# Linear attention and a gated FFN on one core: blocks 4 and 5 get all their scalings on ScalarE, with loads and casts dealt anew

## The chip, the cores and the metric

The kernel runs on one core of a Trainium2 chip. The core has TensorE (PE in the profile; PEld is its loading of weights), VectorE (DVE), ScalarE (ACT), GpSimd (POOL) and SyncE (SP), which here only issues DMAs. Each engine runs its own instructions in order; semaphores tie the engines together. The metric is device time of one launch in microseconds (us), lower is better. Runs before: 319.34, 318.82 and 317.79 us, median 318.82.

## The reference

Eight batches of eight heads, 576 positions, head size 64, in float32. The attention is linear: q and k are clipped at zero and scaled by a cosine and a sine of the position, side by side, so that a head has 128 features.

```
def phi(x, c, s):
    r = np.maximum(x, 0.0)
    return np.concatenate([r * c, r * s], axis=-1)
kv = np.einsum('bhsf,bhsd->bhfd', k_p, v)
z = np.sum(k_p, axis=2)
num = np.einsum('bhsf,bhfd->bhsd', q_p, kv)
den = np.einsum('bhsf,bhf->bhs', q_p, z)[..., None] + 1e-06
return (num / den)
```

Its result, as 4608 tokens of 512 numbers, goes through a gated FFN with 1536 hidden columns: `(gelu(x @ w_gate) * (x @ w_val)) @ w_out`.

## The kernel before, in words

**Two rhythms.** Attention goes by batch (576 tokens, eight batches b), the FFN by block of 512 tokens (nine blocks n). While block n's FFN runs on PE, the attention of batch n + 1 is made in its gaps, and the loading and scaling of batch n + 2. Block n has 12 units `jt`, each 128 hidden columns; a loop over n and jt calls the helpers in an order written out by hand (the scheduler is off), so that the order of calls is the order on each engine.

**A batch's way.** SP loads q, k and v of a batch into the staging tile `st` (`load`, L98), as 128 partitions x 4 head pairs m x 9 position columns j x 64. Each column j is then scaled twice, with the cosine table (part 0, "c") and the sine table (part 1, "s"), into the bf16 tile `phis`: `prep` for one name (L177 on ACT, L179 on DVE) or `prep_both` for q and k in one instruction (L191 on ACT, L193 on DVE). v is cast into `vx` (`cast_v`, L208). From batch 2 on, two DMA transposes (`turn_q`, L222), one for each half of the partitions, turn the scaled q into `qT`. `kv_unit` (L270) makes the key-value sums. `nm_unit` (L311, then DVE at L322 to L324) makes the numerators of 128 positions, divides them and writes `x_sb`; even and odd heads read the two halves of `qT`, so it needs both transposes. `turn_x` (L378) turns x by DMA into the FFN's input `xT`.

**Staging.** `st` has three places. From batch 4 on, q and k of the next batch land on top of those of the last, so a load of columns waits until these columns of the batch before have been scaled. q of batch 4 has its own load at slot (2, 1), in two halves by head pair.

**The FFN.** Up to block 3 a unit is `gv_unit` (L430): gate matmuls into one PSUM bank, value matmuls into another, a Gelu on ACT (L439) and a product on DVE (L442). Blocks 4 and 5 are made of four groups each (`group`): a pair of units by seven products of the Strassen kind (`Pair`, p1 to p7, matmuls at L650) and one ordinary unit. On the way, ACT copies sums (L669, L673) and makes Gelus (L682, L686), and DVE adds and multiplies (L677, L690, L691, L695). The product p4 writes into the bank that L690 reads, so it waits for L690, which waits for the Gelu at L686. From block 6 on there are pairs alone.

**The output product** of the block before is also made by seven products (`product`, L547), one a slot or two. Their PSUM pieces of 128x256 are partly copied to `sm` on ACT (L565), added up on DVE (L560) and stored by `flush` (L453). POOL makes the sums of hidden activations (`h_sum`, L529) and of x (`x_sum`, L630).

**The slots.** In blocks 4 and 5 a group calls three slots x, y and z, for jt = 3g, 3g + 1 and 3g + 2. A slot makes an output product (`o_step`), then attention's part: transposes of x, loads (`LOADS`), at jt = 0 the q transposes, at jt = 1 the kv unit, and the scalings that `PREPS` names for that jt. In `PREPS`, "s3" is the sine of column 3 on ACT, "c5" the cosine of column 5 on ACT, and a capital "C" the cosine on DVE; keys "C0" and "C3" are called at the ends of groups 0 and 3. In block 3 the scalings of batch 5 stand in `COMING`, over slots 7 to 11, the last with column 8 in slot 11.

**SP's queue around block 4**, from the profile's order: two stores, the first parts of q and k of batch 6 (slot 9 of block 3), three x transposes, two stores (slot 10), two loads of v, the second parts of q and k (slot 0 of block 4), the two q transposes of batch 5.

The lines that order SP's loads and the scalings are these:

```
(3, 9): [(6, "q", 0, 4), (6, "k", 0, 4)],
(4, 0): [(6, "q", 4, R), (6, "k", 4, R)], (3, 11): [(6, "v")],
(4, 9): [(7, "q", 0, 4), (7, "k", 0, 4), (7, "v")],
(5, 0): [(7, "q", 4, R), (7, "k", 4, R)],
PREPS = {
    2: "s0 s1", 3: "s2", 4: "C2 C3", 5: "s3 s4", 6: "c4", 7: "s5",
    8: "c5 s6", 9: "s7", 10: "c6", 11: "s8 c7", "C0": "C0 C1", "C3": "C8",
}
```

Of the kernel before, what the change touches and what calls it, by code (L numbers as in the profile page):

```python
# [16 lines left out]
def kernel(  # L17
# [13 lines left out]
    nc = tc.nc  # L31
# [3 lines left out]
    C = H * D  # L35
# [4 lines left out]
    R = S // 64  # L40
# [118 lines left out]
    act_copy, dve_copy = nc.scalar.copy, nc.vector.tensor_copy  # L159
# [47 lines left out]
    def cast_v(b, m0, m1, copy, j0=0, j1=R):  # L207
        copy(  # L208
            vx[:, m0:m1, j0:j1, 0:D],
            staged["v", b][:, m0:m1, j0 * D:j1 * D].rearrange("p m (j d) -> p m j d", d=D),  # L210
        )
# [243 lines left out]
    def flush(engs=(nc.sync, nc.sync)):  # L455
        for i, o_sb in stores:
            store(engs, i, o_sb)
        stores.clear()
# [76 lines left out]
    got = {}  # L535
    LEFT, RIGHT = slice(0, CH), slice(CH, C)

    def product(n, p, i, u, m, v):


        a, b = PROD[i]
        key = n, p
        at = {1: u, 6: u, 7: u, 5: m, 3: m, 2: v, 4: v}[i]
        last = n == NB - 1
        joint = not last and n > 2
        for j in range(JH):
            nc.tensor.matmul(  # L547
                at,
                lhsT=hs.setdefault(key, h_parts(n, p))[a][:, j],
                rhs=ts[b][:, j],  # L550
                start=(j == 0 and i in ((1, 2, 4, 5), (1, 4, 5))[joint]),
                stop=(j == JH - 1),
                skip_group_check=i in (3, 6, 7) or joint and i == 2,
            )
        if key not in got:
            got[key] = [outp.tile([128, C], FP32, name="o_sb") for _ in range(2)]
        lo, hi = got[key]

        def add(o, k, x, op=ALU.add):
            nc.vector.tensor_tensor(o, got[key, k], x, op=op)  # L560

        if i in (6, 7) or i == (2 if joint else 1) or last and i == 5:
            k, of = (1, u) if i == 2 else (i, at)
            got[key, k] = place(n, p, f"u{k}", CH, FP32)
            nc.scalar.copy(got[key, k], of)  # L565
        if i == (2 if last or joint else 1):
            add(lo[:, LEFT], 1, v)
        if i == 7:
            add(hi[:, RIGHT], 7, got[key, 5] if last else m)
        if i == 4:  # L570
            add(hi[:, LEFT], 7, v, ALU.subtract)
        if i == 3:
            add(lo[:, RIGHT], 6, m)
        if last and p == 1:

            if i == 2:
                store((nc.sync, nc.sync), 4 * n + p, lo, 0, CH)
            if i == 4:
                store((nc.sync, nc.gpsimd), 4 * n + 2 + p, hi)
            if i == 3:  # L580
                store((nc.sync, nc.scalar), 4 * n + p, lo, CH, C)
        elif i in (3, 4):
            flush()
            stores.append((4 * n + 2 + p, hi) if i == 4 else (4 * n + p, lo))
            if last:
                flush()
# [113 lines left out]
    def group(n, g, x, y, z):  # L700

        f = Pair(n, g, g % 2, 1 - g % 2, g % 2)
        f.p1()
        numerators(n, 3 * g)
        f.p5()
        x()
        f.p6()
        numerators(n, 3 * g + 1)
        f.p2()
        y()  # L710
        f.p3()
        f.p7(MIX)

        def between():
            numerators(n, 3 * g + 2)
            z()
            f.p4()

        gv_unit(n, 8 + g, to=(2, 2), between=between)
        preps(n, f"C{g}")  # L720

    def fast_step(new, old, a=None, b=None):

# [127 lines left out]
    for m in (0, 2):  # L851
# [6 lines left out]
        + [("q", 0, 2, 4, 2), ("o", 2, 0), ("q", 2, 4, 4, 3), ("o", 3, 0), ("o", 0, 4)]  # L858
        + [("q8", 2), ("o", 1, 4), ("o", 2, 4), ("kv",)]
        + [("o", 3, 4)]  # L860
        + [("nm", 0, 2), ("o", 0, 8), ("nm", 1, 6), ("o", 1, 8), ("xt", 0, 4), ("nm", 2, 2), ("q2", 0, 2)]
        + [("q2", 2, 3), ("o", 2, 8), ("xt", 1, 5), ("nm", 3, 6), ("q2", 3, 4)]
        + [("o", 3, 8)]
        + [("xt", 2, 4)]
    )
    for what, *a in order:
        if what == "o":
# [29 lines left out]
    def js(a, b):  # L897
# [13 lines left out]
            11: [("qk", 5, js(8, 9))],  # L911
        },
    }
    LOADS = {
        (1, 11): [(3, "k"), (3, "v")],
        (2, 1): [(4, "q")], (2, 6): [(4, "k"), (4, "v")],
        (2, 10): [(5, "k")], (3, 0): [(5, "q")], (3, 1): [(5, "v")],
        (3, 9): [(6, "q", 0, 4), (6, "k", 0, 4)],
        (4, 0): [(6, "q", 4, R), (6, "k", 4, R)], (3, 11): [(6, "v")],
        (4, 9): [(7, "q", 0, 4), (7, "k", 0, 4), (7, "v")],  # L920
        (5, 0): [(7, "q", 4, R), (7, "k", 4, R)],
    }
    SUMS = {
        2: {0: "1", 1: "2", 2: "34", 3: "56", 6: "78"},
# [47 lines left out]
    def start_loads(n, jt):  # L972
        for b, name, *part in LOADS.get((n, jt), ()):
            if part:
# [6 lines left out]
    for n in range(1, 4):  # L981
        b = n + 1

        t_kv, t_nm, t_turn = {1: (7, 9, 12), 2: (6, 7, 11), 3: (2, 5, 9)}[n]
        for jt in range(JT):
            if n == 1 and jt >= t_nm:
                nm_unit(2, jt - t_nm, (6, 4, 6)[jt - t_nm])
                turn_x(2, jt - t_nm)
            heads = (0, 2, 4, 4)[n]
            if jt >= heads:  # L990
                gv_unit(n, jt, to=(2, 6) if (n, jt) == (3, JT - 1) else None)
            else:
                for i in range(2):
                    half, unit = divmod(2 * jt + i, heads)
                    gv_unit(n, unit, half * HALF, HALF)
                    if n == 1:
                        j = JA + 2 * jt + i
                        prep("q", b, 1, (j,), eng=nc.scalar)
                        prep("q", b, 0, (j,))
                        if jt == i == 0:  # L1000
                            turn_x_pe(1, 3, 5, act_copy)
            i = jt - t_nm - 1
            if n > 1 and 0 <= i < late_of(b):
                turn_x(b, i)
            if n > 1:
                o_step(n, jt)
            elif jt % 3 == 1:
                flush()
            if n == 1 and jt == 2:
                prep("q", b, 0, (R - 1,))  # L1010
                prep("q", b, 1, (R - 1,), eng=nc.scalar)
                turn_q(b)
                nm_unit(1, NT - 1)
            if n == 1 and jt == 3:
                turn_x(1, NT - 1)
            nms = [(b, jt - t_nm)] if n > 1 and 0 <= jt - t_nm < NT else []
            if n == 2 and jt < 2:
                nms.append((n, 3 + jt))
            for bt in nms:
                nm_unit(*bt)  # L1020
            if jt == t_kv:
                kv_unit(b)
            if n == 1 and jt in (2, 3, 4):
                prep_third("k", b, jt - 2)
            if n == 1 and jt == 5:
                cast_v(b, 0, 4, dve_copy)
            if (n, jt) in q3:
                cosines, sines_ = q3[n, jt]
                prep("q", 3, 1, sines_, eng=nc.scalar)
                prep("q", 3, 0, cosines)  # L1030
            for name, c, what in COMING.get(n, {}).get(jt, ()):
                if name == "v":
                    cast_v(c, what, what + 2, act_copy if c == 4 else nc.gpsimd.tensor_copy)
                elif name == "qk":
                    for j in what:
                        prep_both(c, 0, j, nc.scalar if j % 2 else nc.vector)
                        prep_both(c, 1, j, nc.scalar)
                else:
                    prep(name, c, 0, what)
                    prep(name, c, 1, what, eng=nc.scalar)  # L1040
            c = {(2, 1): 2}.get((n, jt), b if n > 1 and jt == t_turn else None)
            if c is not None and n < 3:
                turn_q(c + 1)
            start_loads(n, jt)
            c = {(2, 1): 2, (3, 2): 3, (3, 9): 4}.get((n, jt))
            if c is not None:
                for i in range(late_of(c), NT):
                    turn_x(c, i)
            if n == 3 and 3 <= jt < 7:
                w_sum(("S2", "S2", "S4", "S4")[jt - 3], (1 - jt % 2) * 512, (2 - jt % 2) * 512)  # L1050
            if n == 1 and 4 <= jt < 8:
                wo_sum(("T3", "T1", "T2", "T4")[jt - 4])
            more(n, jt)
# [1 line left out]


    PREPS = {
        2: "s0 s1", 3: "s2", 4: "C2 C3", 5: "s3 s4", 6: "c4", 7: "s5",
        8: "c5 s6", 9: "s7", 10: "c6", 11: "s8 c7", "C0": "C0 C1", "C3": "C8",
    }  # L1060
    turns = []

    def preps(n, jt):
        b = n + 1
        if 4 <= b < B - 1:
            for what in PREPS.get(jt, "").split():
                eng = nc.vector if what[0] == "C" else nc.scalar
                prep_both(b + 1, "cs".index(what[0].lower()), int(what[1]), eng)

    def numerators(n, jt):  # L1070
        b, t = n + 1, {6: 0, 7: 1, 9: 2, 10: 3, 0: 4}.get(jt)
# [110 lines left out]
```

## Time and profile before

| | |
|---|---|
| median of the runs | 318.82 us (317.79 to 319.34) |
| the profiled execution | 316.06 us |
| its span, first to last instruction | 314.3 us |
| mean granted TensorE clock | 0.997 |
| PE busy | 299.2 us (95%) |
| DVE busy | 235.5 us (75%) |
| ACT busy | 191.8 us (61%) |
| POOL busy | 139.4 us (44%) |
| scalings at L193 (DVE) | 15, mean 907 ns, 477 to 1756 |
| scalings at L191 (ACT) | 39, mean 715 ns |
| copies at L565 into `sm` (ACT) | 42, mean 372 ns |
| DVE `o_sb` sums at L560 waiting for ACT's copies | 14.6 us in 17 waits |

The profile is of one execution, which took 316.06 us: 314.3 from the first to the last instruction and 1.8 around it. Busy time is what an engine spends in its instructions; a matmul's end is modelled, so a busy PE isn't PE at its peak. In the views of a timeline a line has the start and the time in us, the engine, the source line, the operation, the tile written and the tiles read, and how many instructions are merged; a bracket holds the idle time ahead of it and who ended that. Block 4 runs from about 147 to 180 us, block 5 to about 213.

### The profile page before, as it was taken

The page shows a single profiled execution, that of the slowest core. Times are in us where ns is not written, and L with a number is a line of the kernel's source. Part 1 is how long each engine was busy: PE and PEld are TensorE (multiplying, and loading weights), DVE is VectorE, ACT ScalarE, POOL GpSimd, SP SyncE. Part 2 cuts the span into 40 slices and gives each one's busy share as a digit, 9 for nine tenths or more (in the row PEclk, how much of TensorE's full clock was granted, in tenths as well). Part 3 has the DMA queues.
Part 4 walks back from the last instruction along what each step waited for, and adds up shares of the span by engine and source line. Part 5 has one row for each costly group of instructions (what it writes and reads, how often), then busy time and mean ns, then how long its engine had stood idle before and what let it go on. Part 6 is the DMA issues. An engine that isn't in the chain of part 4 may idle for free.

```text
span 314.3 us, 7893 instructions
## 1 busy us (share of the span) xinstructions
PE 299.2 (95%) x3055; PEld 223.3 (71%) x3055; DVE 235.5 (75%) x507; ACT 191.8 (61%) x397; POOL 139.4 (44%) x120
## 2 busy tenths in 40 slices
PE   8899999999999999999979997899999999999993
PEld 3574556654866578666757776678899888888882
DVE  5855896699897795989687858676679786756772
ACT  7864766957463756269657857485655465565530
POOL 6774420000030000028855396476975777197420
PEclk9999999999999999999999999999999999999998
DMA  7999999883799979998994699637741512113035
GB/s 276 256 183 263 295 333 390 253 130 60 246 170 222 311 210 211 260 242 208 322 174 94 191 269 208 125 63 95 113 101 37 101 33 46 36 33 67 2 78 126
DMA packets 71126, 53.67 MB, mean 171 GB/s; under 512 B 45392, under 2 KB 58448, under 8 KB 71088
## 3 DMA queue, kind: packets, MB, share of 16 engines
q1 hardware_dynamic: 61312, 41.17, 56.8%
q0 software_dynamic: 9696, 11.93, 16.5%
q8 instruction: 24, 0.39, 0.5%
q14 instruction: 14, 0.11, 0.1%
q10 hardware_dynamic: 80, 0.07, 0.1%
HBM read 37.75 MB, written 9.44 MB: 150 GB/s over the span
## 4 chain that ended last, share of the span: by engine, by line
PE 74%; DMA 7%; ACT 6%; issue 5%; DVE 4%; SPq 2%; POOL 1%; POOLq 0%; DVEq 0%; ACTq 0%
PE ps L430 24%; PE ps L650 23%; PE ps L547 16%; PE ps L311 3%; PE ps L463 3%; DMA st<-in_v_dram 2%; PE ps L270 2%; DMA st<-in_q_dram 2%; DMA qT<-phis 2%; ACT phis L177 2%; ACT phis L191 1%; SPq L222 1%; SPq L98 1%; PE ps L233 1%; PE ps L401 1%
## 5 line engine op out<-in xcount | busy, mean ns | idle before, releaser
L430 PE MATMUL ps<-xT,wg_sb 128*128 128x512 bf16 (+1 forms) x256 | 57.2, 346 | 1.2 <-ACT xT L390 0.6
L430 PE MATMUL ps<-xT,wv_sb 128*128 128x512 bf16 (+1 forms) x256 | 57.2, 346 | 0.0
L439 ACT ACTIVATE gel<-ps 128x512 f32<-128x512 f32 (+1 forms) x64 | 33.8, 531 | 26.9 <-PE ps L430 25.3
L442 DVE TENSOR_TENSOR hT<-gel,ps 128x512 bf16<-128x512 f32 (+1 forms) x64 | 38.0, 601 | 16.1 <-PE ps L430 12.0
L208 POOL CAST vx<-st 128x1152 bf16<-128x1152 f32 x8 | 10.2, 1281 | 88.1 <-DMA st<-in_v_dram 44.9
L529 POOL TENSOR_TENSOR sm<-hT 128x768 bf16<-128x768 bf16 x20 | 33.1, 1656 | 23.3 <-PE ps L650 16.4
L430 PEld LDWEIGHTS <-wv_sb 128*128 128x128 bf16 x256 | 25.0, 98 | 20.2
L547 PEld LDWEIGHTS <-sm 128*128 128x128 bf16 x336 | 32.8, 98 | 7.4 <-DVE sm L529 0.5
L430 PEld LDWEIGHTS <-wg_sb 128*128 128x128 bf16 x256 | 23.5, 98 | 16.1 <-issue 1.8
L650 PE MATMUL ps<-fs,ws 128*128 128x256 bf16 x240 | 34.5, 273 | 0.2 <-ACT ps L669 0.2
L560 DVE TENSOR_TENSOR o_sb<-sm,ps 128x256 f32<-128x256 f32 x56 | 23.4, 419 | 15.0 <-ACT sm L565 14.6
L177 ACT ACTIVATE phis<-st,sin_t 128x256 bf16<-128x256 f32 (+1 forms) x75 | 31.5, 485 | 4.2 <-DMA st<-in_q_dram 3.4
L650 PEld LDWEIGHTS <-ws 128*128 128x128 bf16 x320 | 30.2, 98 | 4.1 <-ACT ps L669 0.5
L690 DVE TENSOR_TENSOR ps<-fs,ps 128x512 f32<-128x512 f32 x26 | 18.1, 695 | 20.0 <-PE ps L650 13.7
L547 PEld LDWEIGHTS <-hT 128*128 128x128 bf16 x288 | 28.2, 98 | 5.4
L682 ACT ACTIVATE gel<-ps 128x512 f32<-128x512 f32 x26 | 15.5, 597 | 26.4 <-PE ps L650 26.4
L650 PE MATMUL ps<-xT,wg_sb 128*128 128x256 bf16 x208 | 31.2, 273 | 0.0
L324 DVE TENSOR_TENSOR x_sb<-ps,rec 128x512 bf16<-128x512 f32 x38 | 26.3, 692 | 1.3
L565 ACT COPY sm<-ps 128x256 f32<-128x256 f32 x42 | 15.6, 372 | 17.2 <-PE ps L547 16.6
L547 PE MATMUL ps<-wo_sb,hT 128*128 128x256 bf16 x192 | 23.7, 273 | 0.0
L547 PE MATMUL ps<-T,sm 128*128 128x256 bf16 x168 | 22.9, 273 | 0.3 <-DVE sm L529 0.3
L547 PE MATMUL ps<-wo_sb,sm 128*128 128x256 bf16 x168 | 22.9, 273 | 0.0
(124 smaller groups left out, 565.5 us busy)
## 6 DMA issues: line engine op xcount, KB each, us to landing
out_dram<-o_sb SPq DMA_DIRECT2D x69, 128.0 KB, 2.4
st<-in_v_dram SPq DMA_DIRECT2D x12, 576.0 KB, 6.7
st<-in_k_dram SPq DMA_DIRECT2D x8, 576.0 KB, 4.7
st<-in_q_dram POOLq DMA_DIRECT2D x4, 576.0 KB, 12.5
st<-in_q_dram SPq DMA_DIRECT2D x4, 576.0 KB, 5.3
st<-in_q_dram SPq DMA_DIRECT2D x3, 640.0 KB, 6.8
st<-in_q_dram SPq DMA_DIRECT2D x3, 512.0 KB, 4.0
wg_sb<-in_moe_w_gate_dram POOLq DMA_DIRECT2D x6, 256.0 KB, 7.0
```

Source lines behind the costliest of these rows:

```text
L177: nc.scalar.activation(o, i, AF.Relu, scale=tab[:, j:j + 1])
L324: nc.vector.tensor_tensor(x, nm[:, :, :, 0:D], rec[:, :, :, None].to_broadcast([128, 2, 4, D]), op=ALU.mult,)
L430: nc.tensor.matmul(bank(to[g])[:, 0:w], lhsT=wt[:, ct, js], rhs=xt[:, ct, c0:c0 + w], start=(ct == 0), stop=(ct == CT - 1),)
L439: nc.scalar.activation(gel[:, 0:w], bank(to[0])[:, 0:w], AF.Gelu)
L442: nc.vector.tensor_mul(hT[n][:, jt, c0:c0 + w], gel[:, 0:w], bank(to[1])[:, 0:w])
L529: eng.tensor_tensor(a[name][:, j0:j1], a[x][:, j0:j1], a[y][:, j0:j1], op=op)
L547: nc.tensor.matmul(at, lhsT=hs.setdefault(key, h_parts(n, p))[a][:, j], rhs=ts[b][:, j], start=(j == 0 and i in ((1, 2, 4, 5), (1, 4, 5))[ ...
L560: nc.vector.tensor_tensor(o, got[key, k], x, op=op)
L565: nc.scalar.copy(got[key, k], of)
L650: nc.tensor.matmul(to[:, 256 * half:256 * half + 256], lhsT=w_part(a, j * 128, (j + 1) * 128)[:, ct], rhs=xb[self.n][b][:, ct], start=(hal ...
L682: nc.scalar.activation(self.gel0, self.other, AF.Gelu)
L690: nc.vector.tensor_tensor(bank(val), self.m5, self.sum, op=ALU.add)
```

## The change

It has five parts; TensorE's own order isn't touched.

- `PREPS` is written anew: in blocks 4 and 5 all 18 scalings of a batch go to ACT, one for each gap between ACT's other instructions (two after the unit's Gelu). A new key "m0" to "m3" stands in each group after p7, ahead of the ordinary unit's Gelu; "C0" and "C3" go.
- The copies at L565 for the output products of blocks 3 and 4, which are made during blocks 4 and 5 (six in each), go from ACT to DVE.
- The loads of q and k of batches 6 and 7 are split five columns to four instead of four to five, and the first part of batch 6 moves from slot 9 to slot 10 of block 3, behind the x transposes and stores there.
- Batch 4's q is loaded in two parts by column (0 to 3, then 4 to 8) instead of by head pair.
- The casts of v: batch 3's two go from POOL to ACT, batch 4's second from ACT to DVE. In the order ahead of block 1, two pairs of q scalings of batch 2 move behind the last x^T copy.

```diff
-            nc.scalar.copy(got[key, k], of)
+            (dve_copy if n in (3, 4) else act_copy)(got[key, k], of)
...
         f.p7(MIX)
+        preps(n, f"m{g}")
...
         gv_unit(n, 8 + g, to=(2, 2), between=between)
-        preps(n, f"C{g}")
...
-        + [("nm", 0, 2), ("o", 0, 8), ("nm", 1, 6), ("o", 1, 8), ("xt", 0, 4), ("nm", 2, 2), ("q2", 0, 2)]
-        + [("q2", 2, 3), ("o", 2, 8), ("xt", 1, 5), ("nm", 3, 6), ("q2", 3, 4)]
+        + [("nm", 0, 2), ("o", 0, 8), ("nm", 1, 6), ("o", 1, 8), ("xt", 0, 4), ("nm", 2, 2), ("q2", 0, 1)]
+        + [("o", 2, 8), ("xt", 1, 5), ("nm", 3, 6), ("q2", 1, 2)]
         + [("o", 3, 8)]
-        + [("xt", 2, 4)]
+        + [("xt", 2, 4), ("q2", 2, 4)]
...
+    casts = {
+        (3, 0): act_copy, (3, 2): act_copy, (4, 0): act_copy, (4, 2): dve_copy,
+        (5, 0): nc.gpsimd.tensor_copy, (5, 2): nc.gpsimd.tensor_copy,
+    }
...
-        (2, 1): [(4, "q")], (2, 6): [(4, "k"), (4, "v")],
+        (2, 1): [(4, "q", 0, 4), (4, "q", 4, R)], (2, 6): [(4, "k"), (4, "v")],
...
-        (3, 9): [(6, "q", 0, 4), (6, "k", 0, 4)],
-        (4, 0): [(6, "q", 4, R), (6, "k", 4, R)], (3, 11): [(6, "v")],
-        (4, 9): [(7, "q", 0, 4), (7, "k", 0, 4), (7, "v")],
-        (5, 0): [(7, "q", 4, R), (7, "k", 4, R)],
+        (3, 10): [(6, "q", 0, 5), (6, "k", 0, 5)],
+        (4, 0): [(6, "q", 5, R), (6, "k", 5, R)], (3, 11): [(6, "v")],
+        (4, 9): [(7, "q", 0, 5), (7, "k", 0, 5), (7, "v")],
+        (5, 0): [(7, "q", 5, R), (7, "k", 5, R)],
...
-                    cast_v(c, what, what + 2, act_copy if c == 4 else nc.gpsimd.tensor_copy)
+                    cast_v(c, what, what + 2, casts[c, what])
...
-        2: "s0 s1", 3: "s2", 4: "C2 C3", 5: "s3 s4", 6: "c4", 7: "s5",
-        8: "c5 s6", 9: "s7", 10: "c6", 11: "s8 c7", "C0": "C0 C1", "C3": "C8",
+        "m0": "s0", 2: "c0 s1", 3: "c1", 4: "s2", "m1": "c2", 5: "s3 c3", 6: "s4", 7: "c4",
+        "m2": "s5", 8: "c5 s6", 9: "c6", 10: "s7", "m3": "c7", 11: "s8 c8",
...
-                eng = nc.vector if what[0] == "C" else nc.scalar
-                prep_both(b + 1, "cs".index(what[0].lower()), int(what[1]), eng)
+                prep_both(b + 1, "cs".index(what[0]), int(what[1]), nc.scalar)
```

## The prediction

> **What bounds the kernel now.** I began with the page's slices of the span: TensorE (PE) is at nine tenths nearly throughout and its clock is granted in full, so only its gaps can be won.
>
> ```profile
> PE   8899999999999999999979997899999999999993
> PEclk9999999999999999999999999999999999999998
> ```
>
> Each digit is 7.9 us. Beyond the start and the tail, the dips are at 157 and at 189 to 204 us. Next I listed PE's instructions in order of time and kept those with idle time before them; the bracket names who ended it.
>
> ```profile
> 54.74 0.60 PE L430 MATMUL ps<-xT,wg_sb 128*128 128x256 bf16 x4 [0.41 <-ACT xT L390]
> 89.22 0.83 PE L547 MATMUL ps<-T,sm 128*128 128x256 bf16 x6 [0.25 <-DVE sm L529]
> 107.71 0.42 PE L311 MATMUL ps<-kv_sb,qT 128*128 128x65 bf16 x8 [0.69 <-DVE x_sb L324]
> 119.67 0.60 PE L430 MATMUL ps<-xT,wg_sb 128*128 128x256 bf16 x4 [0.46 <-ACT gel L439]
> 162.99 0.60 PE L650 MATMUL ps<-fs,wv_sb 128*128 128x256 bf16 x4 [1.69 <-DVE ps L690]
> 195.93 0.60 PE L650 MATMUL ps<-fs,wv_sb 128*128 128x256 bf16 x4 [1.69 <-DVE ps L690]
> 198.95 0.40 PE L311 MATMUL ps<-kv_sb,qT 128*128 128x65 bf16 x7 [1.09 <-DMA qT<-phis]
> ```
>
> With 0.18 at 57.05 and 0.23 at 148.43, that is 6.7 us: all that this change can reach. Third, the timeline around the two large gaps.
>
> ```profile
> 159.12 1.64 POOL L529 TENSOR_TENSOR sm<-hT 128x768 bf16<-128x768 bf16 x1
> 159.68 2.65 DVE L193 TENSOR_SCALAR phis<-st,cos_t 128x512 bf16<-128x512 f32 x2
> 160.70 1.35 POOL L208 CAST vx<-st 128x1152 bf16<-128x1152 f32 x1
> 162.25 0.68 DVE L690 TENSOR_TENSOR ps<-fs,ps 128x512 f32<-128x512 f32 x1
> 180.47 0.48 DVE L193 TENSOR_SCALAR phis<-st,cos_t 128x512 bf16<-128x512 f32 x1
> ```
>
> A cosine scaling on DVE takes 0.48 us while POOL rests and some 1.3 beside it; two of them keep L690, and so PE's fourth product, waiting. The same stands at 192.63. Last, SyncE's (SP's) DMA queue, with the q transposes of batches 5 and 6 and, from each window, how long they and the loads before them took to land.
>
> ```profile
> 141.99 0.40 SPq L98 DMA_DIRECT2D st<-in_q_dram  x1
> 146.92 1.18 SPq L453 DMA_DIRECT2D out_dram<-o_sb  x2
> 148.19 1.09 SPq L98 DMA_DIRECT2D st<-in_v_dram  x2
> 150.85 11.29 SPq L222 DMA_TRANSPOSE qT<-phis  x2
> L222 SPq DMA_TRANSPOSE qT<-phis x2: 3757/5618/7478, 150.8 to 158.4; - x2
> DMA to landing us min/median/max: 6.3/8.1/9.9
> L222 SPq DMA_TRANSPOSE qT<-phis x2: 3794/5876/7957, 184.5 to 192.5; - x2
> DMA to landing us min/median/max: 6.4/8.3/10.1
> ```
>
> The second transpose of batch 5 is issued at 158.4 and lands 6.3 later, at 164.7; the numerators that need it start at 164.72. For batch 6 it is 192.5 + 6.4 = 198.9, and PE resumes at 198.95. So behind each 1.69 gap a DMA lands at or after PE's arrival: taking the gap away alone lets PE wait there for the transpose. In both cases the first transpose is held on the queue until the last load before it has landed (load of k: 150.3 + 8.0 = 158.3, transpose over at 158.33; 183.9 + 8.6 = 192.5, over at 192.45), and the second lands 6.4 after that. What is loaded just ahead of a q transpose therefore sets it.
>
> **The order before block 1** (q2 scalings). Two sine/cosine pairs move behind the x^T copy that PE waited for at 54.74. ACT goes from 51.94 to 59.4 with no flagged idle, and the copies of the next piece (56.59, PE at 57.05) stand behind the same set of ACT instructions in both orders: two scalings of 0.50, two copies, a Gelu. PE would start 0.41 earlier and wait 0.41 more there: 0. Bounds: -0.59 (both gaps gone) to +0.5 (one scaling more ahead).
>
> **v casts.** Batch 3's two casts go from POOL (1.14, 1.54) to ACT, where the row of batch 4's is 1.14 each. On DVE the L529 sum beside a POOL cast took 1.47 for two at 87.70 (0.55 apiece elsewhere), ending in the 0.25 gap: -0.25. On ACT they stand before the Gelus of units 5 and 6; ACT was idle 0.59 and 1.58 there, the banks are wanted two units (over 4 us) later, and the casts would be over by about 96.8, before the kv unit at 97.78: hidden. Cover gone: up to +1.1 at that unit. Batch 4's second cast goes from ACT (1.15) to DVE (0.77), after the 0.46 gap, which stays with the first cast: 0, bounds -0.46 to +0.77.
>
> **Batch 4's q in two parts by column.** The two loads by head pair left SP at 95.97 and 97.39 and landed 4.8 and 6.6 later; ACT's first scaling needed both, waited 3.38 us to 104.11, held a Gelu up, and PE lost 0.69. The first part (512 KB, columns 0 to 3) has all that slot 7 needs, and by the first row lands near 100.8, about when ACT comes free (100.73): -0.69. Bounds -0.69 to 0; slots 8 and 9 wait for the second part with slack.
>
> **Scalings and copies in blocks 4 and 5.** Off DVE: five L193 a block (in block 4: 0.88 for two, 2.65 for two, 0.48 = 4.0 us). Onto ACT: five L191 at 0.715 = 3.6. Off ACT: six L565 at 0.372 = 2.2. Onto DVE: six copies of a 128x256 PSUM piece, a form that DVE has no row for; bounds 0.28 (its 128x130 kv cast from PSUM) and 0.42 (L560, same size and source); I take 0.41, as L560 is nearest: 2.5. ACT gains 1.3 us a block of 32, DVE loses 1.5. Neither is the bound: ACT was busy 21.9 of the 32 us from 148 to 180. One gap by hand, group 1: L682 at 158.3, scaling to 159.6, Gelu L686 to 160.2 (0.6 later than now), L690 to 160.95; PE asks for it at 161.30. So both 1.69 gaps go: -3.38, if nothing stands behind them.
>
> [...]
>
> **Loads five to four.** The first parts (q and k, five columns, 640 KB each) may not leave before column 4 is scaled, and move from slot 9 to slot 10. On SP they are so moved past three x transposes and two stores: from 141.99 to the end of the stores. These wait for the sum at 145.95 (0.41) on DVE, so leave near 146.4 and end near 147.6. Before, these two loads (512 KB each) had landed by 147.3 in an otherwise idle stretch; now all six loads go out between 147.6 and the transposes, whose issue (150.85, behind the last column's scaling) stays. That is 1.05 MB more in the same queue, begun 0.6 us earlier. At the two v loads' rate (landed 152.1 and 153.6: 590 KB in 1.5 us, 0.39 MB/us) it costs 2.7 us, net +2.1: qT at 166.8, where PE now would come at 163.03. Bounds: +1.2 (the first 0.4 us of issue and more overlap) to +5.2 (0.18 MB/us, as the two 640 KB loads before batch 6's transpose moved from 185.2 to 192.5: 5.8 less 0.6). I take 2.1, the plain-load rate, since most of it goes before the transposes begin.
>
> [...]
>
> The first scaling in block 4 wants k's five columns: issued near 148.1, landing 4.9 to 8.3 later by the rows of its kind, 153.0 to 156.4, against 153.45 before the unit's Gelu is late. That wait, up to 3.0, lies in front of the qT wait and is hidden by its 3.8; uncovered it would count.
>
> In block 5 the order on SP stays; 262 KB go with the early loads instead of just ahead of the transpose (0.67 us), and the last cosine no longer sits before the numerators on DVE (0.27). PE, freed of its gap, waits for qT until 0.7 earlier than now (bounds 0 to 0.94).
>
> **Sum**, against the profiled execution (span 314.3, 1.8 around it, 316.06): -0.25 - 0.69 + 2.1 - 0.7 = +0.5, so 316.5. That execution is 0.9% under the median of the runs; in proportion, 318.82 x 316.5/316.06 = 319.3.
>
> **Rivals.** *The transpose isn't behind the loads* (0.24). If the six loads delay nothing, block 4 stays at 164.72 and the sum is -1.6: 317.2. If besides a q transpose takes the 12.7 us of batch 7's (215.83 to 222.1 and 228.5, no load near), qT lands at 163.6 and 196.9: -0.94 - 1.2 - 2.0 = -4.1, 314.7. For it: transposes of batches 2 and 3 took 10.7 and 11.2. Against: two holds that end with the last load. *The six loads crawl* (0.16): a slower kernel, one place, qT of batch 5 in block 4, priced at 0.18 MB/us: -0.94 + 5.2 - 0.7 = +3.6, 322.4; it decides once that qT lands over 3.2 us later than now. For it: the 182 to 192 stretch; against: 0.39 before. *ACT too full* (0.08): a scaling before each Gelu makes L690 late, 0.2 to 0.7 in four groups that no qT wait covers, +0.8 to +2.8 on the sum: 320 to 322. Against: the slack above, 0.35.
>
> **How the numbers follow.** The likeliest case has 0.52; its own range is 318.1 to 321.1: -0.94 + 1.2 - 0.94 = -0.7, and, with the 0.69 not won and the transpose 3.2 later, -0.25 + 3.2 - 0.7 = +2.25. Half a percent (1.6 us) is about what a measurement here can tell from no change. Of the 0.52, 0.09 lies above 320.4 (half a percent up); of the first rival 0.02, and of the last 0.01, lies within. Faster 0.22; same 0.43 + 0.02 + 0.01 = 0.46; slower 0.09 + 0.16 + 0.07 = 0.32. The range 315.6 to 322.6 leaves out the far ends.
>
> **What would show it.** Right: no PE wait on L690; a PE wait on qT of 2 to 5 us at the first numerators in block 4 and 2 to 3 in block 5; no 0.69 gap at the old 107; ACT's first block-4 scaling waiting for k. Wrong: no wait on qT in block 4 (then the transfers overlapped, and the kernel is faster), or waits on Gelus instead.

## The result, and the profile after

| | before | after |
|---|---|---|
| median (20 runs each, same chip) | 317.98 us (315.78 to 319.92) | 320.57 us (317.24 to 323.72) |
| ratio, 95% interval | | 1.006 (1.0034 to 1.0087) |
| the profiled execution | 316.06 us | 318.89 us |
| its span, granted clock | 314.3 us, 0.997 | 317.1 us, 0.994 |

The kernel became slower by 0.6%, some 1.9 us. Runs over 1.5% above the fastest of their kernel, five of the 20 after and four of the 12 of e3_scalings below, are left out of the ratios; the two medians hold all 20 runs, which is why they stand 2.6 us apart.

The slices of the span of the changed kernel, as shown of the one before (7.9 us a digit):

```profile
PE   8889999899999999999968999799999999999993
PEclk9999999999999999999997999999999999999999
```

The dip at 189 to 204 us is shallower, a deeper one has come at 158 to 174, and the clock's row has a 7 in the middle: TensorE (PE) ran slower in part of that slice. (The 8 that ends the row of the kernel before lies behind PE's last work; see below.) Next, PE's instructions in order of time (start, length, idle time before and who ended it), from block 2 to block 5 of the changed kernel:

```profile
113.68 0.61 PE L430 MATMUL ps<-xT,wg_sb 128*128 128x256 bf16 x4 [0.26 <-DMA xT<-x_sb]
119.90 0.60 PE L430 MATMUL ps<-xT,wg_sb 128*128 128x256 bf16 x4 [0.58 <-ACT gel L439]
...
163.42 0.20 PE L311 MATMUL ps<-kv_sb,qT 128*128 128x65 bf16 x1
167.28 0.57 PE L311 MATMUL ps<-kv_sb,qT 128*128 128x65 bf16 x7 [3.65 <-DMA qT<-phis]
167.65 1.04 PE L650 MATMUL ps<-fs,ws 128*128 128x256 bf16 x4
168.49 1.49 PE L547 MATMUL ps<-wo_sb,sm 128*128 128x256 bf16 x6
...
201.95 0.40 PE L311 MATMUL ps<-kv_sb,qT 128*128 128x65 bf16 x7 [2.23 <-DMA qT<-phis]
```

Both 1.69 us waits on L690 are gone, and the 0.69 us wait near 107 too. In their place PE waits 3.65 and 2.23 us for `qT`. What follows the first of these is new: four L650 matmuls take 1.04 us and six L547 1.49, where the same rows elsewhere read 0.60 and 0.82. The same stretch cut into pieces of 2 us (columns: us; busy us and count of PE, PEld, DVE, ACT, POOL; then the granted clock, the DMA share and GB/s):

```profile
164.00:166.00 2.00, 0.00 (x0) 0.00 (x0) 0.00 (x0) 0.00 (x0) 0.00 (x0) 1.00 0.98 135
166.00:168.00 2.00, 0.72 (x9) 0.66 (x10) 0.12 (x1) 0.00 (x0) 0.00 (x0) 0.66 0.92 175
168.00:170.00 2.00, 2.00 (x12) 1.34 (x10) 0.94 (x3) 1.21 (x2) 0.00 (x0) 0.50 0.62 130
170.00:172.00 2.00, 2.00 (x25) 1.82 (x24) 1.74 (x5) 0.70 (x2) 1.88 (x2) 0.99 0.36 69
```

While PE waited, its clock was halved, and it came back only at 170 us. From the seven numerators that waited to the start of the next 12-fold L547 PE took 3.76 us (167.28 to 171.04); before, with all eight, it took 2.48 (164.72 to 167.20). That is 1.3 us more. SP's queue ahead of the wait, with the transposes' time from issue to landing:

```profile
147.52 0.55 SPq L98 DMA_DIRECT2D st<-in_q_dram  x1
148.12 0.53 SPq L98 DMA_DIRECT2D st<-in_k_dram  x1
148.75 1.16 SPq L98 DMA_DIRECT2D st<-in_v_dram  x2
150.06 0.44 SPq L98 DMA_DIRECT2D st<-in_q_dram  x1
...
L222 SPq DMA_TRANSPOSE qT<-phis x2: 3777/6668/9558, 151.2 to 160.8; - x2
DMA to landing us min/median/max: 6.4/9.3/12.2
```

All six loads now go out between 147.5 and 151.1. The last of them (k, issued at 150.55) landed 10.2 us later, at 160.75; there the first transpose's instruction ends too (151.2 + 9.56), and the second lands 6.4 later, at 167.2, when PE resumes.

In block 4 of the kernels e2 to e4 below the first transpose's instruction ends at 162.8, 158.8 and 160.4 us, and PE resumes 6.3 to 6.9 us after that.

To compare kernels stage by stage I take the start of the key-value unit (L270) of each batch from PE's timeline, called kv2 to kv7. From kv5 to kv6 is in the main block 4, from kv6 to kv7 block 5.

| us | start to kv1 | kv1 to kv2 | kv2 to kv4 | kv4 to kv5 | kv5 to kv6 | kv6 to kv7 | kv7 to end |
|---|---|---|---|---|---|---|---|
| before | 46.87 | 22.64 | 52.68 | 28.53 | 32.94 | 34.21 | 96.4 |
| after | 48.41 | 22.63 | 51.37 | 28.53 | 36.43 | 33.37 | 96.4 |

Block 4 lost 3.5 us. The 1.5 us ahead of kv1 belong to code that the change doesn't touch; over the thirteen executions profiled it ranges from 46.9 to 49.9.

### The profile page after: what moved, and what is told of

Its sections match the earlier page's. It is cut to its first block, busy times and chain, and to the rows that moved or that the text cites. A ratio compares the mean times of both kernels' runs of the same rounds, so it can differ in the third digit from the quotient of the medians.

```text
span 317.1 us, 7856 instructions
## 1 busy us (share of the span) xinstructions
PE 299.1 (94%) x3032; PEld 224.4 (71%) x3055; DVE 232.4 (73%) x510; ACT 194.6 (61%) x396; POOL 135.8 (43%) x118
## 4 chain that ended last, share of the span: by engine, by line
PE 76%; DMA 11%; issue 4%; ACT 4%; POOL 1%; SPq 1%; DVE 1%; POOLq 0%; DVEq 0%
PE ps L430 25%; PE ps L650 23%; PE ps L547 18%; DMA qT<-phis 4%; PE ps L270 3%; PE ps L463 3%; PE ps L311 3%; DMA st<-in_v_dram 2%; DMA xT<-x_sb 2%; DMA wv_sb<-in_moe_w_val_dram 2%; ACT phis L177 1%; ACT phis L191 1%; POOL st L529 1%; PE ps L401 1%; PE ps L233 1%
## 5 line engine op out<-in xcount | busy, mean ns | idle before, releaser
L430 PE MATMUL ps<-xT,wg_sb 128*128 128x512 bf16 (+1 forms) x240 | 54.5, 344 | 2.6 <-ACT xT L390 0.7
L208 POOL CAST vx<-st 128x1152 bf16<-128x1152 f32 x6 | 7.1, 1179 | 89.1 <-DMA st<-in_v_dram 89.1
L547 PEld LDWEIGHTS <-sm 128*128 128x128 bf16 x336 | 33.2, 99 | 7.1
L650 PE MATMUL ps<-fs,ws 128*128 128x256 bf16 x240 | 35.1, 276 | 0.2 <-ACT ps L669 0.2
L650 PEld LDWEIGHTS <-ws 128*128 128x128 bf16 x320 | 30.5, 99 | 4.4 <-ACT ps L669 0.5
L682 ACT ACTIVATE gel<-ps 128x512 f32<-128x512 f32 x26 | 15.5, 597 | 28.7 <-PE ps L650 28.7
L547 PEld LDWEIGHTS <-hT 128*128 128x128 bf16 x288 | 28.2, 98 | 5.4
L690 DVE TENSOR_TENSOR ps<-fs,ps 128x512 f32<-128x512 f32 x26 | 18.1, 696 | 18.0 <-PE ps L650 13.7
L650 PE MATMUL ps<-xT,wg_sb 128*128 128x256 bf16 x208 | 31.2, 273 | 0.0
L529 POOL TENSOR_TENSOR sm<-hT,sm 128x768 bf16<-128x768 bf16 x10 | 16.4, 1642 | 17.3 <-PE ps L547 15.0
L547 PE MATMUL ps<-wo_sb,hT 128*128 128x256 bf16 x192 | 23.7, 273 | 0.0
L547 PE MATMUL ps<-wo_sb,sm 128*128 128x256 bf16 x168 | 23.6, 278 | 0.0
L547 PE MATMUL ps<-T,sm 128*128 128x256 bf16 x168 | 22.9, 273 | 0.1
```

Of the source, the lines that this page charges most:

```text
L430: nc.tensor.matmul(bank(to[g])[:, 0:w], lhsT=wt[:, ct, js], rhs=xt[:, ct, c0:c0 + w], start=(ct == 0), stop=(ct == CT - 1),)
L529: eng.tensor_tensor(a[name][:, j0:j1], a[x][:, j0:j1], a[y][:, j0:j1], op=op)
L547: nc.tensor.matmul(at, lhsT=hs.setdefault(key, h_parts(n, p))[a][:, j], rhs=ts[b][:, j], start=(j == 0 and i in ((1, 2, 4, 5), (1, 4, 5))[ ...
L650: nc.tensor.matmul(to[:, 256 * half:256 * half + 256], lhsT=w_part(a, j * 128, (j + 1) * 128)[:, ct], rhs=xb[self.n][b][:, ct], start=(hal ...
L682: nc.scalar.activation(self.gel0, self.other, AF.Gelu)
L690: nc.vector.tensor_tensor(bank(val), self.m5, self.sum, op=ALU.add)
```

## The experiments

The theory was that `qT` lands a fixed time after the last load queued ahead of its transposes, that this takes back what the scalings win, and that the lower clock after the long wait adds 1.3 us. The rivals: the scalings win nothing in any case; the lower clock costs nothing; the loads, not the transposes behind them, are what costs. The results, in the same stages (qT waits of blocks 4 and 5 as the timeline gives them):

| kernel | ratio to before | kv2 to kv4 | kv5 to kv6 | kv6 to kv7 | qT waits |
|---|---|---|---|---|---|
| before | 1 | 52.68 | 32.94 | 34.21 | 0, 1.09 |
| after | 1.006 (1.0034 to 1.0087) | 51.37 | 36.43 | 33.37 | 3.65, 2.23 |
| e1_old_loads | 1.0021 (0.9989 to 1.0054) | 52.32 | 34.92 | 33.48 | 2.15, 2.35 |
| e2_new_loads | 1.0087 (1.0061 to 1.0113) | 52.84 | 35.02 | 34.23 | 1.89, 1.11 |
| e3_scalings | 1.0017 (0.999 to 1.0044) | 52.13 | 35.21 | 34.44 | 2.52, 3.31 |
| e4_turn_first | 0.987 (0.9846 to 0.9893) | 53.55 | 32.65 | 30.96 | 1.51, 0 |
| h1_plain_before | 0.9865 (0.9786 to 0.9945) | 50.93 | 32.94 | 32.95 | 0, 0 |
| h2_plain_after | 0.9925 (0.9892 to 0.9958) | 50.93 | 35.91 | 30.96 | 2.89, 0 |
| h3_plain_scalings | 0.9831 (0.9749 to 0.9914) | 50.93 | 32.25 | 33.22 | 1.12, 1.88 |
| h4_plain_loads | 0.9948 (0.9908 to 0.9989) | 50.93 | 34.89 | 32.95 | 1.61, 0 |
| i1_plain_busy | 0.9909 (0.9874 to 0.9944) | 50.93 | 34.92 | 33.05 | 0.74, 1.77 |
| i2_plain_turn_first | 0.9777 (0.9741 to 0.9812) | 50.93 | 32.19 | 30.97 | 0.29, 0 |
| i3_plain_turn_first_old | 0.9893 (0.9861 to 0.9924) | 50.92 | 32.95 | 32.94 | 0, 0 |

**e1_old_loads**: the changed kernel with batch 6's loads as before.

```
-        (3, 10): [(6, "q", 0, 5), (6, "k", 0, 5)],
-        (4, 0): [(6, "q", 5, R), (6, "k", 5, R)], (3, 11): [(6, "v")],
+        (3, 9): [(6, "q", 0, 4), (6, "k", 0, 4)],
+        (4, 0): [(6, "q", 4, R), (6, "k", 4, R)], (3, 11): [(6, "v")],
```

> The changed kernel, but batch 6's q and k are loaded as before: four columns at slot 9 of block 3, five at slot 0 of block 4. My theory (the second q transpose of batch 5 lands 6.4 us after the last load queued ahead of it, and PE's first numerators of block 4 wait for it): the last load lands near 158.3, qT near 164.8, PE's wait there falls from 3.65 to some 1.5 us, the clock stays at 1.00 behind it, and from batch 5's kv unit to batch 6's it is about 33.0 us in place of 36.4; ratio to the kernel before about 0.995. Rival (ACT, now with all scalings, is the loss): these loads change nothing, 36 us and a ratio of 1.004 to 1.008.

Block 4 came down by 1.5 us against the changed kernel, by the wait alone (3.65 to 2.15). The clock fell here too, behind the shorter wait. Two pieces of 2 us of this kernel, same columns as above:

```profile
166.00:168.00 2.00, 1.97 (x16) 1.46 (x17) 1.06 (x3) 0.71 (x2) 0.00 (x0) 0.58 0.93 206
168.00:170.00 2.00, 2.00 (x18) 1.57 (x17) 0.93 (x2) 0.50 (x1) 1.31 (x1) 0.57 0.36 70
```

PE waited from 163.9 to 166.0 and ran from 166.3 to 169.7 at half clock. So the expectation missed in the clock, and in the wait (2.15 us, not 1.5). By block 4 here, in e2 and in h4 the loads are worth 1.5 to 2.1 us.

**e2_new_loads**: the kernel before with only that load change, the same lines the other way round.

> The kernel before with nothing but batch 6's loads dealt anew (five columns at slot 10 of block 3, four at slot 0 of block 4). My theory: qT of batch 5 lands 2 to 2.5 us later than before and PE waits for it at block 4's first numerators, behind the 1.69 us gap that stays; 35 to 36.5 us from kv unit 5 to kv unit 6 (32.9 before), ratio 1.006 to 1.010. Rival (the scalings are the loss, not the loads): 33 us and 1.000.

As the theory had it. The 1.69 us waits stay, and a wait for qT stands behind the first (kernel e2_new_loads, PE in order of time):

```profile
165.40 0.60 PE L650 MATMUL ps<-fs,wv_sb 128*128 128x256 bf16 x4 [1.69 <-DVE ps L690]
169.22 0.40 PE L311 MATMUL ps<-kv_sb,qT 128*128 128x65 bf16 x7 [1.89 <-DMA qT<-phis]
```

Block 4 took 2.1 us more than before (35.02 against 32.94).

**e3_scalings**: the kernel before with only the scalings and copies.

```
-            nc.scalar.copy(got[key, k], of)
+            (dve_copy if n in (3, 4) else act_copy)(got[key, k], of)
...
-        2: "s0 s1", 3: "s2", 4: "C2 C3", 5: "s3 s4", 6: "c4", 7: "s5",
-        8: "c5 s6", 9: "s7", 10: "c6", 11: "s8 c7", "C0": "C0 C1", "C3": "C8",
+        "m0": "s0", 2: "c0 s1", 3: "c1", 4: "s2", "m1": "c2", 5: "s3 c3", 6: "s4", 7: "c4",
+        "m2": "s5", 8: "c5 s6", 9: "c6", 10: "s7", "m3": "c7", 11: "s8 c8",
```

> The kernel before with nothing but the scalings all on ACT and the output-sum copies of blocks 4 and 5 on DVE; loads, casts and orders as before. My theory: both 1.69 us waits on L690 go and PE waits for qT in their place, 1.5 to 1.8 us in block 4 and 2.5 to 3 in block 5; 32.7 to 33.0 us from kv unit 5 to 6, ratio 0.998 to 1.001. Rival one (the gaps were what bound it): 3.4 us less, ratio 0.989. Rival two (ACT too full): over 33.5 us and a ratio above 1.004.

The waits on L690 went, and both came back as waits for qT (kernel e3_scalings, same view):

```profile
165.14 0.56 PE L311 MATMUL ps<-kv_sb,qT 128*128 128x65 bf16 x7 [2.52 <-DMA qT<-phis]
201.13 0.40 PE L311 MATMUL ps<-kv_sb,qT 128*128 128x65 bf16 x7 [3.31 <-DMA qT<-phis]
```

Block 4 took 35.21 us, longer than before: its wait is longer than the 1.5 to 1.8 us expected, and the clock fell from 165.0 to 168.4, which wasn't foreseen. No wait for a Gelu is seen there, so the "over 33.5 us" of rival two isn't ScalarE's. The ratio says that nothing was won, as expected; over all its 12 runs the mean is 320.3 us against 318.3 before, at a mean clock of 0.989.

**e4_turn_first**: the changed kernel with the q transposes ahead of the loads of the same slot.

```
-        start_loads(n, jt)
         b = n + 1
         if jt == 0 and b < B:
             turn_q(b)
+        start_loads(n, jt)
```

> The changed kernel with the q transposes put on SP's queue ahead of the second parts of the next q and k loads (two lines of attention() change places). My theory: the last load ahead is then v's, landing near 158, so qT of batch 5 lands near 164.3 (PE waits under 1.2 us, no lower clock) and in block 5 near 197, with no wait; the second parts land near 167, in time or up to 1 us late for the scaling of column 5. 32 to 33 us from kv unit 5 to 6, ratio to before 0.985 to 0.992. Rival (the transposes are slow of themselves, whatever is ahead of them): waits as in the changed kernel, ratio 1.004.

It beats both kernels, by 1.3% the one before. In block 5 no wait is left, in block 4 one of 1.51 us (under 1.2 was expected) behind the loads of v and of the first parts, which are still ahead. The clock's row of its page:

```profile
PEclk9999999999999999999999999999999999999999
```

**The four with plain copies** (h1 to h4) take the transposes away. Every DMA transpose becomes plain copies of as many bytes:

```
-            nc.sync.dma_start_transpose(
-                out=qt_tile(b)[:, i].rearrange("f m (j p) -> f (m j) p", p=64),
-                in_=phi["q", b][64 * i:64 * i + 64].rearrange("p m j f -> p (m j f)"),
-            )
+            for a in range(2):
+                nc.sync.dma_start(
+                    out=qt_tile(b)[64 * a:64 * a + 64, i].rearrange("f m s -> f (m s)"),
...
-            nc.sync.dma_start_transpose(
-                out=xT_block(blk)[:, :, c:c + m], in_=x[o:o + m, :]
-            )
+            for a in range(128 // m):
+                nc.sync.dma_start(
+                    out=xT_block(blk)[m * a:m * a + m, :, c:c + m],
```

In their profiles later lines are shifted: L222 is L223, L311 is L314, L650 is L655, L690 is L695.

> The kernel before with every DMA transpose (of q into qT and of x into xT) replaced by plain copies of as many bytes, so that qT and xT hold untransposed data and the output isn't the reference's. It is the ground for the next three. Both theories: the copies land some 2 to 4 us after their issue, no wait on qT is left, both 1.69 us waits on L690 stay, ratio to the kernel before 0.985 to 0.998.

> The changed kernel with the same replacement (the output isn't the reference's). Theory (the change takes twice 1.69 us and some 1.3 us of blocks 1 to 3 off TensorE, and the transposes that land after the loads give it all back): ratio lower than that of h1_plain_before by 0.012 to 0.016, no wait on L690, granted clock 1.00 throughout. Rival (something else in the change costs as much, such as ScalarE's load or the loads themselves): lower by at most 0.004.

> The kernel before with the scalings on ScalarE and the output-sum copies on VectorE alone, and the same replacement (the output isn't the reference's). Theory (the scalings are worth the two 1.69 us waits, 3.4 us, wherever qT isn't what comes last; with the transposes e3_scalings gained nothing): ratio lower than that of h1_plain_before by 0.009 to 0.012. Rival (the waits behind VectorE move to ScalarE or to another instruction of VectorE): lower by at most 0.003.

> The kernel before with batch 6's loads split five to four in the later slot alone, and the same replacement (the output isn't the reference's). Theory (the 0.9% that e2_new_loads cost came only through the transposes that stood behind the later loads): the same ratio as h1_plain_before within 0.003. Rival (the later loads cost by themselves, by traffic or by the scalings that wait for them): higher by 0.006 to 0.010.

h1 behaves as said, but "some 2 to 4 us after their issue" was wrong: without any transposing the copies of q took 11 us too. The copies of batch 5's q, first of h1, then of h4 (issue ns, first and last start; below, us to landing):

```profile
L223 SPq DMA_DIRECT2D qT<-phis x4: 488/588/594, 150.5 to 152.3; - x4
DMA to landing us min/median/max: 11.0/11.4/11.6
```

```profile
L223 SPq DMA_DIRECT2D qT<-phis x4: 587/592/2139, 152.4 to 155.8; - x4
DMA to landing us min/median/max: 11.6/11.7/12.9
```

So what stood on this queue behind the loads landed late whatever its kind (11.0 to 12.9 us), and with the later loads it also left later (one issue took 2.1 us). In h4 block 4 took 34.89 us against 32.94 in h1: the load change costs 1.95 us without a transpose in sight. The theory that it costs only through the transposes falls, and the rival holds. That rests on the stage: the ratios (0.9948, 0.9865) lie apart as the rival said, but their intervals touch.

h2 fell on the rival's side: 0.6% above h1, not 1.2% or more below it, since its copies, too, were waited for in block 4 (1.73 and 1.16 us, with a clock fall after them). Its block 5, where no wait was left, took 30.96 us against 32.95. h3 won 0.7 us in block 4 and lost 0.3 in block 5 (waits of 1.12 and 1.88); its ratio is 0.3% below h1's with intervals of 0.8% each way, and decides nothing.

**i1_plain_busy**: h2 with work for PE in the wait of block 4.

```
         if t is not None and b > 4:
+            if (b, t) == (5, 0):
+                dummies(12, 6)
             nm_unit(b, t)
```

> The changed kernel with plain copies in place of the transposes (h2_plain_after, the output isn't the reference's), and 12 matmuls of 128x512 whose results are never read put on TensorE just ahead of block 4's first numerators, inside its wait for qT (12 x 0.22 = 2.6 us of the 1.73 + 1.16 us). Theory (the clock falls because TensorE stands idle through most of one 3.4 us stretch, and each fall costs some 1.4 us): no fall in block 4, mean granted clock of its runs 0.998 or more instead of 0.994, from the kv unit of batch 5 to that of batch 6 about 34.6 us instead of 35.9, ratio 0.987 to 0.990 instead of 0.9925. Rival (the fall has another cause, or costs nothing in the end): clock 0.994, 35.9 us, ratio 0.992 or more.

The clock held. First pieces of 1 us of h2, which fall just after its wait, then PE's timeline and pieces of 2 us of i1:

```profile
166.00:167.00 1.00, 1.00 (x8) 0.73 (x7) 0.86 (x2) 1.00 (x2) 0.16 (x1) 0.60 0.00 0
167.00:168.00 1.00, 1.00 (x13) 0.80 (x12) 0.50 (x2) 0.10 (x1) 1.00 (x1) 0.50 0.05 10
```

```profile
163.10 2.75 PE L157 MATMUL ps<-ws 128*128 128x512 bf16 x12
165.69 0.19 PE L314 MATMUL ps<-kv_sb,qT 128*128 128x65 bf16 x1
166.62 0.39 PE L314 MATMUL ps<-kv_sb,qT 128*128 128x65 bf16 x7 [0.74 <-DMA qT<-phis]
```

```profile
166.00:168.00 2.00, 1.38 (x18) 1.30 (x19) 0.89 (x3) 0.52 (x2) 0.00 (x0) 1.00 0.07 24
168.00:170.00 2.00, 2.00 (x26) 1.82 (x25) 1.85 (x6) 1.36 (x4) 1.75 (x2) 1.00 0.26 51
```

qT came 0.6 us later than in h2 (the wait ends 16.1 us after kv5, there 15.5), yet the block took 34.92 us instead of 35.91. That is the theory's direction and most of its size, from one profile of each kernel. In the whole time the gain isn't resolved: 0.9909 against 0.9925, since block 5 had waits of 0.66 and 1.11 us here and none in h2, by the same code, and its runs' mean clock, 0.9955, was hardly above h2's 0.994 (in its profiled run, at 0.995, matmuls near the start were slow: 36 of L250 took 1.17 us at 12.1 and 0.75 at 10.5).

**i2_plain_turn_first and i3_plain_turn_first_old**: h2 and h1 with the copies of q ahead of the loads, as in e4_turn_first.

> The changed kernel with plain copies in place of the transposes, and the copies of q issued ahead of the loads of the same step (the output isn't the reference's). Theory (the change is worth 2.0 us in a block where qT is in time: block 5 of h2_plain_after took 30.96 us from kv unit to kv unit where h1_plain_before took 32.95): 30.9 to 31.3 us in both blocks or a short wait left in block 4, clock 0.997 or more, no waits on L690, ratio 0.975 to 0.982. Rival (VectorE or ScalarE bounds these blocks once qT is in time, so that block 4 keeps 32.9 us): ratio 0.986 or more.

> The kernel before with plain copies in place of the transposes, and the copies of q issued ahead of the loads of the same step (the output isn't the reference's). Theory (without the change the scalings on VectorE hold TensorE back 1.69 us in each block, however early qT is): both 1.69 us waits stay, 32.9 us in both blocks as in h1_plain_before, ratio 0.985 to 0.990, so some 3 to 4 us above i2_plain_turn_first. Rival (early qT is all that matters): 31 us in both blocks, ratio within 0.003 of i2_plain_turn_first.

These set the whole change against the kernel before where q is early. PE's waits in blocks 4 and 5, first i2, then i3:

```profile
154.84 1.02 PE L435 MATMUL ps<-xT,wv_sb 128*128 128x512 bf16 x4 [0.61 <-ACT gel L444]
163.37 0.40 PE L314 MATMUL ps<-kv_sb,qT 128*128 128x65 bf16 x7 [0.29 <-DMA qT<-phis]
```

```profile
163.36 0.60 PE L655 MATMUL ps<-fs,wv_sb 128*128 128x256 bf16 x4 [1.69 <-DVE ps L695]
196.31 0.60 PE L655 MATMUL ps<-fs,wv_sb 128*128 128x256 bf16 x4 [1.69 <-DVE ps L695]
```

With q in time the old scalings hold PE 1.69 us in each block, and the new ones don't: 310.85 against 315.17 us on the same chip, 1.2% of the time before between the ratios. By stages it is 2.0 us in block 5 and 0.8 in block 4, where 0.61 goes to a late Gelu and 0.29 to q. Of the 4.3 us between the medians these are 2.8; another 0.9 in the two profiles lies ahead of kv1, which the change doesn't touch. Early q alone won nothing over h1 (0.9893 and 0.9865, intervals overlapping): there was no wait to win.

Four more kernels with the transposes in place were planned (f1 to f4, then g1 to g4), and there is no result of any: the changed kernel with PE kept busy in its waits, the early parts of the change alone, the kernel before with the q transposes ahead of the loads, and e4_turn_first with v's load moved behind as well. So how much of e4's 1.3% the order of the transposes would win without the scalings is open; the kernel before waits 1.09 us for qT in block 5.

## Why the prediction was right or wrong

The forecast was no change that can be told, 319.3 us, in a range of 315.6 to 322.6. The median is 320.57, in the range but just over the 320.4 from which the prediction counts a run as slower; the ratio, 0.6%, says the same. The likeliest case is what happened, in its places, but a term was missing from its sum. That the time came so near is partly luck: the forecast stands on 318.82, the median of three runs, and 20 runs give 317.98; the forecast change was +0.5 us, the measured one 1.9 to 2.6.

- **The waits move to qT: right.** No wait on L690; 3.65 us on qT in block 4 where 3.8 stood in the working, 2.23 in block 5 where 2 to 3 stood.
- **Loads five to four, +2.1: right in size.** qT came at 167.2 (166.8 said), in a run whose kv5 is 0.22 later. Alone it costs 2.1 us of block 4 (e2). The last k landed 10.2 us after its issue, 8.0 before. It is the queue, though, not the transposing: h4 pays 1.95 with plain copies.
- **Block 5, -0.7: right**, 34.21 to 33.37, -0.84.
- **Scalings, -3.38 "if nothing stands behind them": right**, with something behind them they won nothing (e3); without, the whole change won 2.8 us in blocks 4 and 5 (i2 against i3). The copies on DVE took 0.42 each (0.41 said). Of the rival that ScalarE is too full, priced at 0.8 to 2.8 us, 0.61 us (i2) and 0.30 (i1) of waiting for a Gelu in block 4 is all that was seen.
- **First scaling on k: right**, ACT waited for it and PE did not:

```profile
153.82 0.72 ACT L191 ACTIVATE phis<-st,sin_t 128x512 bf16<-128x512 f32 x1 [0.36 <-DMA st<-in_k_dram]
```

- **Order before block 1, 0: right**; kv1 to kv2 took 22.64 and 22.63. The 0.41 us wait reappears in a later one of 0.75.
- **v casts -0.25 and batch 4's q -0.69: not shown.** The weak step is that each was read from one wait of one execution. In the profile after, kv2 to kv4 is 1.3 us shorter, which seems to confirm them and more. But e1 and e4 have the same early parts and took 52.32 and 53.55, e2 and e3 have the old ones and took 52.84 and 52.13. The 0.25 us wait is in neither e2 nor e3, so it wasn't a lasting cost of the old casts; the 0.69 is in e2 and not in e3. What moves most between these executions is how late the transposes of x land (PE waited 0.26, 0.76 and 2.03 us for `xT` in the three with the new parts, 0.55 in e3). The means, 52.4 with the new parts and 52.6 with the old, lie closer than the executions of either do, and decide nothing. With plain copies the stretch takes 50.93 us with old and new parts alike, but there the 0.69 us wait is absent with the old parts too (h1, i3), so this doesn't test the term. (The working reads the row at 87.70 as two sums; it is one of 1.47 us. The term doesn't use it.)
- **The clock: missing.** This is the step that failed: the working has PE resume at full speed after a 3.8 us wait, and puts the clock at nothing without a reason. The price is 1.3 us in the profiled run. Over the 20 runs of the changed kernel the mean granted clock comes in steps:

| mean granted clock of the run | runs | median us |
|---|---|---|
| 1.000 | 1 | 317.2 |
| 0.994 to 0.995 | 9 | 319.8 |
| 0.988 to 0.989 | 4 | 320.9 |
| 0.983 to 0.984 | 5 | 322.3 |
| 0.978 | 1 | 323.7 |

A step of 0.0054 is 3.4 us at half clock in a span of 317. A straight line through the 20 gives 1.37 us a step and 318.2 us (standard error 0.4) without any; through the 15 of the ratio, 1.2 and 318.4. The mean is 1.8 steps a run, 2.5 us by the line, and the means of all runs lie 2.6 us apart (318.05 and 320.70): by the line the falls are the whole loss.

The clock of the kernel before, 0.997 in the mean over its 53 runs beside the experiments, can't be priced in this way. In those runs a step goes with only 0.2 us (standard error 0.3), and in its profile all that is lost of the clock lies behind PE's last work, at 309.2 us, where it costs nothing (kernel before, pieces as above):

```profile
310.00:312.00 2.00, 0.00 (x0) 0.00 (x0) 0.00 (x0) 0.00 (x0) 0.00 (x0) 1.00 0.82 214
312.00:314.00 2.00, 0.00 (x0) 0.00 (x0) 0.00 (x0) 0.00 (x0) 0.00 (x0) 0.52 0.01 4
```

So the clock is to be added to the sum with up to 2.5 us: 0.5 + 2.5 = 3.0 as forecast otherwise, 3.9 with the early parts at 0, where 1.9 (1.1 to 2.8) by the ratio and 2.6 by the means were measured. Where the falls beyond the one in block 4 lie in the slower runs no profile shows. That the falls cause the loss is argued from the line, since in the changed kernel, e1 and e3 block 4 had both a fall and the wait's own length (3.65, 2.15 and 2.52 us); only i1 took a fall away while PE still had to wait for qT, and that in the kernel with plain copies.

Of the rivals, "the transpose isn't behind the loads" is out: in block 4 the first transpose ended as the last load ahead of it landed, at 158.3 us before and at 160.75 after, and in e2 the loads alone brought that end to 162.8. "The six loads crawl" is out as priced (+5.2): the wait was 3.65.

## What to carry to other kernels

Ask of a wait that is to be removed what lands next, and on which queue it stands: here 3.4 us of scalings were worth nothing until two lines that put the q transposes ahead of the loads were swapped, and then the whole gave 1.3%. A wait of TensorE may cost more than its own length: behind 2.15 us in e1 came 3.4 us at half clock, behind 3.31 in block 5 of e3 none; fill it or shorten it. And a short wait seen in one execution behind a DMA is no term of a sum before other executions show it too.

## What the runs showed of the hardware

**A fall of the clock lasted 3.4 us, whatever the wait**: 166.6 to 170.0 in the changed kernel, 166.3 to 169.7 in e1, 165.0 to 168.4 in e3, 12.2 to 15.6 in e2, each at half clock (0.50). One followed e1's 2.15 us wait in block 4, and none e3's 3.31 in block 5 (pieces of 2 us of e3_scalings, the clock third from the end):

```profile
198.00:200.00 2.00, 0.00 (x0) 0.00 (x0) 0.16 (x1) 0.41 (x1) 0.00 (x0) 1.00 1.00 144
200.00:202.00 2.00, 0.86 (x13) 0.81 (x14) 0.37 (x2) 0.00 (x0) 0.00 (x0) 1.00 0.89 179
```

PE's work just ahead doesn't divide the cases either. In the 3.4 us before a fall PE was busy for 0.3 us in the changed kernel, 1.0 in e3, about 1.3 in e1 and 1.7 in e2; in the 3.4 us up to the end of e3's wait in block 5, at 201.1, it was busy for 0.1, and the clock stayed at 1.00 to 206. What decides whether the clock falls is not shown.

**A plain copy inside the chip's memory landed late behind loads, as a transpose does**: 11.0 to 12.9 us from issue to landing behind the loads of v, q and k (h1, h4, block 4), 8.6 to 9.0 and 6.6 to 7.7 behind those of q and k alone (h1 and h2, block 5). The first of two transposes kept the queue 7.2 to 9.6 us behind loads (before, after, e2, e3), 4.7 to 4.9 with none just ahead (batch 7's, before and after).
